# A gated linear recurrence followed by a squared-ReLU feed-forward: GpSimd left out from block 9 on, wider zero products, and another written order

## The chip, the cores and the metric

The kernel runs on one core of one Trainium2 chip. The metric is the device time in microseconds (us). Three runs of the kernel before took 178.39, 179.05 and 180.15 us; their median is 179.05 us. One more execution was profiled: it took 179.38 us by the same clock, and its span from the first to the last instruction is 177.7 us. TensorE's granted clock was 1.00 over that span.

## The reference

```python
# q, k, v, alpha: (4, 8, 768, 48) float32; w_in (384, 2048), w_out (2048, 384), s and b scalars
for t in range(S):
    state = alpha[:, :, t, :, None] * state + einsum('bhd,bhe->bhde', k[:, :, t], v[:, :, t])
    y[:, :, t] = einsum('bhd,bhde->bhe', q[:, :, t], state)
x = y.transpose(0, 2, 1, 3).reshape(B * S, H * D)      # 3072 x 384
h = x @ w_in
r = maximum(h, 0.0)
g = s * (r * r) + b
out = g @ w_out                                         # 3072 x 384, float32
```

## The kernel before

The 3072 rows are cut into 24 blocks of 128 (4 batches of 6 blocks; the state starts anew with each batch). Blocks 0 to 5 are loaded and prepared in pairs with interleaved rows, blocks 6 to 23 one by one. The recurrence of a block is done in chunk form:

- loads `a`, `q`, `k`, `v` (alpha and the three inputs, 192 KB each, rows of 192 bytes; line 172, in pairs line 188), six buffers each, all issued by SyncE (SP);
- `ln` (ScalarE, line 324): log of alpha; `cum` (TensorE, lines 335 to 361): running sums by a triangular matrix into PSUM; `eb`, `ei`, `el` (ScalarE, lines 368 to 386): exponentials of them;
- `qb`, `kb` (helper line 234): q and k times these exponentials, two inputs in SBUF. Blocks 0 to 5 are then transposed on TensorE (`T`, line 417) and copied out of PSUM (`Tc`); the others by a DMA transpose (`Td`) from SP;
- `vc`: v cast to bf16; `KV` (lines 439, 451): k by v; `t` and `sn` (lines 464, 466, 234): the new state; `A` (lines 481, 491): the scores; `mk` (lines 502, 508): their mask, PSUM in, 1.22 us on VectorE; `y`, `ya`, `ys` (lines 530, 544, 561): the output, transposed; `ye`: copied out of PSUM as bf16.

The feed-forward takes two blocks at a time. `m` (line 592, 96 of them) is six products of 256 columns into one PSUM bank; `re` (lines 599, 601) its ReLU, `sq` (lines 609, 234) its square into the SBUF ring `gt` that holds 12 blocks. `w` (line 626, 96 of them, the last four on line 618) is four products of 384 columns, a quarter of one block's output sum; `oe` (line 641) adds scale and bias, `st` stores. The weights come as eight loads of 768 KB: `i0` to `i3` (w_in) and `o0` to `o3` (w_out), cast by `ci` and `co` on whichever engine the order names. `ca` to `cd` and `bm` add up w_out's rows for the bias.

All eight PSUM banks are shared by everything; the tables `H_BANK`, `C_BANK` and so on give the bank of each use. `R_BANK` names one of four buffers between `re` and `sq`.

Nothing is scheduled at run time. `ORDER` is one long text of tokens. Each token is a step and a number, with a letter ahead where it runs on another engine than its default (D VectorE, A ScalarE, P GpSimd, S SyncE, T TensorE). The program emits the steps in this order, so each engine's queue holds its own tokens in the order of the text, and every queue is worked off in order: what stands at the head waits, and all behind it with it. The text was written by a planner outside this file.

`z` (line 659) are products of zeros into a bank that is free then. They give nothing to the result; `FILLS` says how many and how wide. TensorE's first one stands at the head of its queue.

Of the kernel before, what the change touches and what calls it, by code (L numbers as in the profile page):

```python
# [51 lines left out]
qb2 T1 KV1 pq2 pk2 KV0 P:kb3 zvp3 A:Tc1 el2 z4 A1 ya0 P:kb2 vc2 t0 mk1 t1 z5 T3 ys1 ya1 ln4 ln5 T2
cum5 i3 Tc3 A:vc3 ye1 KV3 KV2 ye0 Tc2 sn1 A3 cum4 eb5 A2 t2 el5 ei5 mk3 ci0 P:ci1 zs2 pv2 i1 ys2
el4 eb4 ei4 sn2 m0 m1 mk2 ys3 t3 P:ci5 re1 ya3 ya2 D:ci4 re0 sq0 qb5 ye3 ye2 m5 qb4 m4 m8 m9 P:ci7
o0 re5 re4 a6 A:sq4 A:sq5 kb5 sq1 re8 T5 kb4 m13 re13 T4 Tc5 ci6 A:sq13 m12 A5 D:re9 Tc4 D:of0 mk5
m7 sn3 m6 A:sq8 vc5 m15 s0 D:vc4 D:re12 A:sq9 o3 A4 re6 re7 ci2 KV5 KV4 m14 mk4 ci3 A:sq12 o1 o2
re15 m2 ya5 a8 a7 a9 k7 k6 A:sq15 ya4 ys4 t4 D:sn4 ys5 q6 D:co1 D:re14 P:co0 D:re2 D:ye4 v6 m10 m3
w0 w8 sm0 sq7 ln6 q7 v7 k8 sq6 A:sq14 re3 ye5 re10 U0 m21 m16 A:sq10 m11 re21 A:sq21 co7 sq2 sq3
ca0 se0 D:re16 P:co6 cum6 D:co3 el6 re11 A:sq11 ei6 ca3 sq16 m23 m18 w12 m17 m19 re18 ln8 D:re23
D:co2 re19 eb6 re17 ln7 ca1 D:co5 w4 D:co4 cb0 w9 m20 ca2 cb1 kb6 sq17 A:sq18 w13 A:sq19 cc0 qb6  # L60
cd0 D:re20 a11 a10 m22 cum8 w10 w1 cum7 w5 w11 w2 ei8 el8 eb7 ln9 el7 re22 qb7 w6 w14 bm0 w3 eb8
w7 ei7 A:sq22 be0 oe0 sq23 D:vc6 A:sq20 A:vc7 Td6 P:kb7 w20 w16 KV6 w15 w21 cum9 oe2 Td7 q8 t6
ln10 ei9 ln11 oe1 oe3 eb9 w22 A6 A7 w17 w18 w23 mk6 cum10 mk7 y6 y7 q9 KV7 oe5 D:ye7 k9 v9 v8 q10
k10 w19 eb10 ei10 ye6 el10 cum11 m31 el9 t7 oe4 P:qb8 m26 P:qb9 D:re31 kb8 A:vc8 ei11 m25 m24
D:re25 D:re24 m27 A:sq25 m29 eb11 A:sq24 P:kb9 D:re26 P:qb10 k11 Td9 D:re27 D:vc9 P:kb10 A:sq31
KV8 m30 w24 q11 Td8 w28 re30 KV9 A:sq26 a12 sq30 D:re29 sn7 t8 D:sn8 A:sq27 m28 w25 re28 A:sq28
A:sq29 A9 Td10 v10 A8 w29 t9 w26 ln12 mk9 v11 a13 w27 w30 mk8 cum12 y8 y9 A10 P:kb11 w31 P:qb11
ye8 oe6 sn9 D:vc10 el12 ye9 ln13 mk10 vc11 eb12 m37 KV10 Td11 m34 oe7 m36 t10 q13 k13 cum13 k12
a15 D:re34 A11 re36 re37 mk11 m35 ei12 el13 sq36 m39 eb13 m32 sn10 re39 ei13 a14 q12 q14 y11 v13
qb13 sq39 sq37 kb12 ye11 y10 P:kb13 D:re35 ln15 ye10 D:re32 A:sq35 m38 m33 m46 cum15 D:re33 A:sq32  # L70
m44 A:sq33 a17 D:re46 ln14 D:re38 sq38 m45 m42 w36 m41 cum14 Td13 A:sq46 sq34 el15 D:re42 D:re44
ln17 m40 A:sq44 P:qb12 Td12 k14 v12 w37 re45 el14 w38 w39 ei14 eb15 ei15 D:re40 A13 D:vc13 sq45
oe9 A12 A:sq40 mk12 v14 w32 mk13 m43 w33 re41 sq41 a18 a16 w34 A:vc12 eb14 re43 P:kb14 KV12 A:sq43
v15 m47 q15 sq42 t12 w35 A:vc14 ln16 y13 y12 qb14 ye12 w44 D:ye13 re47 cum17 v19 k15 cum16 oe8 k16
eb16 A:sq47 ei17 KV13 P:qb15 m53 v16 Td14 t13 w40 m48 kb15 D:re48 eb17 ln18 el16 re53 ei16 KV14
m55 w41 m52 D:re55 m50 Td15 A:sq55 re52 m54 P:kb16 vc15 w45 KV15 m51 D:sn13 A:sq48 re54 q17 D:re50
t14 D:vc19 A14 mk14 sn14 A:sq50 A15 mk15 t15 w42 w46 A:sq52 q18 A:sq54 w47 m49 y14 re51 y15 oe11
k19 k17 P:qb17 vc16 D:re49 D:sn15 KV16 w43 q16 ye14 ye15 m59 a19 A:sq49 ln19 A:sq51 sq53 qb16 k18
a20 a21 q20 P:kb17 cum18 m57 oe10 w52 m61 Td16 re57 D:re59 Td17 m56 w53 m58 q19 v17 A:sq57 ei18
sq59 D:re61 v18 cum19 ei19 el19 el18 eb18 w54 t16 m63 re58 A:sq61 w55 m62 D:re63 D:re56 sn16 eb19  # L80
P:kb18 sq58 P:kb19 q21 a22 A16 A17 mk17 oe13 ln20 w48 w49 cum20 k20 k23 vc17 w50 m60 w51 D:re62
# [29 lines left out]
def kernel(  # L111
# [15 lines left out]
    B, H, S, D = q.shape  # L127
# [239 lines left out]
    def o_eb(e, u):  # L367
        e.activation(  # L368
            out=b_sb[u % NB].rearrange("a h d -> a (h d)"), in_=BANK[C_BANK[u]][:, 0:384], func=AF.Exp
        )  # L370

    def o_ei(e, u):
        e.activation(  # L373
            out=binv_sb[u % NB].rearrange("a h d -> a (h d)"), in_=BANK[C_BANK[u]][:, 0:384], func=AF.Exp,
            scale=-1.0,
        )

    def o_el(e, u):
        if u < NPB:
            n, g = u - u % 2, u % 2  # L380
            e.activation(
                out=blast_sb[:, n % NBL : n % NBL + 2, 2 * g : 2 * g + 2],
                in_=BANK[C_BANK[u]][:, 384:388].rearrange("a (p c) -> a c p", c=2), func=AF.Exp,
            )
# [386 lines left out]
```

## Time and profile before

| what | value |
|---|---|
| median of three runs | 179.05 us |
| profiled execution: its time, its span | 179.38 us, 177.7 us |
| VectorE busy | 134.0 us (75%), 239 instructions |
| ScalarE busy | 111.3 us (63%), 242 instructions |
| GpSimd busy | 54.6 us (31%), 83 instructions |
| DMA queue 1 (loads, transposes, stores) | 113684 packets, 34.61 MB |
| DMA queue 8 (instructions) | 18 packets, 0.29 MB |

A line of instruction groups gives the source line, the engine, the operation, output<-inputs, the shapes and xcount, then busy us and mean ns of one, then the idle time of the engine just ahead of it and what ended most of that. A timeline line gives start and length in us, the engine and the operation; in brackets the idle time ahead of it and what ended it ("issue" means nothing that the profile shows). "PEld" is TensorE's loading of weights, which overlaps its products.

### The profile page before, as it was taken

The numbers are of one execution on the slowest core, as the hardware profiler recorded it, in microseconds if no ns is written. First come the engines' busy times: TensorE is split into PE (matmuls) and PEld (weight loads), VectorE is DVE, ScalarE is ACT, GpSimd is POOL, SyncE is SP. The second block draws the span as 40 slices with busy tenths as digits, with TensorE's granted clock in tenths as the row PEclk, the third lists the DMA queues.
The fourth block names the chain that finished last, engine by engine and source line by source line (L and its number), as shares of the span: only waits on it lengthen the run. The fifth ranks groups of instructions, "written<-read, shape, count | busy, mean of one in ns | idle before, by whom it ended". The sixth has DMA issues, their size and how long they took to land.

```text
span 177.7 us, 5545 instructions
## 1 busy us (share of the span) xinstructions
PE 169.5 (95%) x2289; PEld 127.7 (72%) x2289; DVE 134.0 (75%) x239; ACT 111.3 (63%) x242; POOL 54.6 (31%) x83
## 2 busy tenths in 40 slices
PE   7898799899999999999999999999999999999992
PEld 7787597677656786687767868767767688877672
DVE  2298889999977999999887789496978779634421
ACT  3867689798662467367686857559649544956000
POOL 7686512400023715214022352634235302000000
PEclk9999999999999999999999999999999999999999
DMA  5999999999799969999989999999979993000352
GB/s 146 325 318 289 271 329 360 313 280 199 141 224 191 200 144 198 146 203 174 192 171 226 128 209 184 197 210 186 207 127 266 185 344 139 4 0 0 141 208 98
DMA packets 113708, 34.96 MB, mean 197 GB/s; under 512 B 106900, under 2 KB 112148, under 8 KB 113684
## 3 DMA queue, kind: packets, MB, share of 16 engines
q1 hardware_dynamic: 113684, 34.61, 87.8%
q8 instruction: 18, 0.29, 0.7%
q14 instruction: 6, 0.05, 0.1%
HBM read 25.17 MB, written 4.72 MB: 168 GB/s over the span
## 4 chain that ended last, share of the span: by engine, by line
PE 71%; DVE 7%; SPq 7%; ACT 6%; DMA 4%; issue 3%; POOL 1%; DVEq 0%; ACTq 0%
PE bank_ps L626 31%; PE bank_ps L592 28%; SPq L188 5%; DMA wst<-in_moe_w_in_dram 4%; PE bank_ps L481 3%; ACT gt L609 2%; PE bank_ps L544 2%; DVE r L601 2%; ACT r L599 2%; PE bank_ps L335 2%; PE bank_ps L530 2%; SPq L258 2%; PE bank_ps L618 1%; DVE am L502 1%; PE bank_ps L439 1%
## 5 line engine op out<-in xcount | busy, mean ns | idle before, releaser
L592 PE MATMUL bank_ps<-xd,w_in_bf 128*128 128x256 bf16 x576 | 72.0, 273 | 1.8 <-DVE r L601 1.1
L626 PE MATMUL bank_ps<-w_out_bf,gt 128*128 128x384 bf16 x368 | 68.1, 326 | 0.0
L592 PEld LDWEIGHTS <-w_in_bf 128*128 128x128 bf16 x576 | 54.5, 98 | 12.2 <-issue 0.9
L626 PEld LDWEIGHTS <-gt 128*128 128x128 bf16 x368 | 34.5, 98 | 19.5 <-issue 0.2
L599 ACT ACTIVATE r<-bank_ps 128x512 bf16<-128x512 f32 x52 | 30.6, 597 | 16.6 <-PE bank_ps L592 11.9
L609 ACT ACTIVATE gt<-r 128x512 bf16<-128x512 bf16 x61 | 36.8, 628 | 5.4 <-DVE r L601 4.9
L601 DVE TENSOR_SCALAR r<-bank_ps 128x512 bf16<-128x512 f32 x44 | 29.3, 685 | 8.9 <-PE bank_ps L592 6.4
L234 POOL TENSOR_TENSOR qk<-k_in,binv 128x384 bf16<-128x384 f32 x16 | 17.0, 1066 | 39.3 <-ACT binv L373 26.6
L502 DVE TENSOR_TENSOR am<-bank_ps,U_bf 128x1024 bf16<-128x1024 f32 x18 | 21.5, 1220 | 4.1 <-PE bank_ps L481 3.6
L234 DVE TENSOR_TENSOR gt<-r 128x512 bf16<-128x512 bf16 x35 | 17.1, 507 | 3.5 <-ACT r L599 3.3
L641 DVE SCALAR_TENSOR_TENSOR wst<-bank_ps,s_col,bias_w 128x384 f32<-128x384 f32 x23 | 14.0, 614 | 6.9 <-PE bank_ps L626 6.4
L234 POOL TENSOR_TENSOR qk<-q_in,b_s 128x384 bf16<-128x384 f32 x13 | 13.4, 1031 | 17.4 <-DMA q_in<-in_q_dram 13.9
L373 ACT ACTIVATE binv<-bank_ps 128x384 f32<-128x384 f32 x24 | 11.9, 498 | 10.3 <-PE bank_ps L342 7.7
L234 POOL TENSOR_TENSOR s_st<-t,blast 128x384 bf16<-128x384 bf16 x11 | 9.4, 855 | 23.7 <-DVE t L466 23.6
L229 ACT ACTIVATE xd<-bank_ps 128x384 bf16<-128x384 f32 x19 | 9.4, 520 | 9.8 <-PE bank_ps L544 9.2
L324 ACT ACTIVATE la<-a_in 128x384 bf16<-128x384 f32 x24 | 12.3, 522 | 5.1 <-DMA a_in<-in_alpha_dram 5.1
L368 ACT ACTIVATE b_s<-bank_ps 128x384 f32<-128x384 f32 x24 | 12.0, 499 | 4.5 <-PE bank_ps L342 3.4
L466 DVE TENSOR_TENSOR t<-bank_ps,s_st 64x192 bf16<-64x192 f32 x32 | 11.3, 352 | 1.7 <-POOL s_st L234 0.6
L234 DVE TENSOR_TENSOR qk<-q_in,b_s 128x384 bf16<-128x384 f32 x11 | 6.0, 550 | 6.3 <-DMA q_in<-in_q_dram 5.9
L659 PE MATMUL bank_ps<-zeros 128*128 128x128 bf16 x81 | 7.2, 255 | 1.3 <-DVE half_bf L695 1.3
L508 DVE TENSOR_TENSOR am<-bank_ps,maskp 128x1024 bf16<-128x1024 f32 x6 | 7.3, 1223 | 0.7 <-PE bank_ps L491 0.6
L530 PE MATMUL bank_ps<-qkT,s_st 128*32 128x128 bf16 x240 | 6.8, 221 | 0.6 <-issue 0.6
(87 smaller groups left out, 156.9 us busy)
## 6 DMA issues: line engine op xcount, KB each, us to landing
out_dram<-wst SPq DMA_DIRECT2D x23, 192.0 KB, 3.1
a_in<-in_alpha_dram SPq DMA_DIRECT2D x18, 192.0 KB, 4.4
k_in<-in_k_dram SPq DMA_DIRECT2D x18, 192.0 KB, 3.9
q_in<-in_q_dram SPq DMA_DIRECT2D x18, 192.0 KB, 3.8
v_in<-in_v_dram SPq DMA_DIRECT2D x18, 192.0 KB, 3.8
wst<-in_moe_w_in_dram SPq DMA_DIRECT2D x4, 768.0 KB, 7.5
wst<-in_moe_w_out_dram SPq DMA_DIRECT2D x4, 768.0 KB, 7.6
a_in<-in_alpha_dram SPq DMA_DIRECT2D x3, 384.0 KB, 4.8
```

What stands on the lines that cost most here:

```text
L234: e.tensor_tensor(out=o, in0=x, in1=y, op=ALU.mult)
L324: e.activation(out=la_sb[u % NLA].rearrange("a (r h) d -> a r h d", r=2)[..., 0:D], in_=seen("a", u), func=AF.Ln,)
L368: e.activation(out=b_sb[u % NB].rearrange("a h d -> a (h d)"), in_=BANK[C_BANK[u]][:, 0:384], func=AF.Exp)
L373: e.activation(out=binv_sb[u % NB].rearrange("a h d -> a (h d)"), in_=BANK[C_BANK[u]][:, 0:384], func=AF.Exp, scale=-1.0,)
L466: e.tensor_tensor(out=t1_sb[n % 2][r, :, c], in0=kv[r, :, c], in1=s_sb[(n - 1) % 3][r, :, c], op=ALU.add,)
L502: e.tensor_tensor(out=am.rearrange("a e p t -> a (e p) t"), in0=a_ps.rearrange("a e p t -> a (e p) t"), in1=U_bf.unsqueeze(1).to_broadcast ...
L592: nc.tensor.matmul(out=hp[:, i * 256 : (i + 1) * 256], lhsT=w_in_bf[:, kk, 128 * j : 128 * (j + 1)], rhs=xd_sb[g % 3][:, kk, :], start=(kk ...
L599: e.activation(out=r_sb[R_BANK[w]], in_=BANK[H_BANK[w]], func=AF.Relu)
L601: e.tensor_scalar_max(r_sb[R_BANK[w]], BANK[H_BANK[w]], 0.0)
L609: e.activation(out=o, in_=r, func=AF.Square)
L626: nc.tensor.matmul(out=BANK[bank][:, 0:d_model], lhsT=gt_sb[:, j, c0 : c0 + C], rhs=w_out_bf[:, j, :], start=(j == 0), stop=(j == NJ - 1),)
L641: e.scalar_tensor_tensor(out=out_sb[n % NOS], in0=BANK[O_BANK[n]][:, 0:d_model], scalar=s_col[:, 0:1], in1=bias_w, op0=ALU.mult, op1=ALU.add,)
```

## The change

Three things change together. The names of banks and buffers are drawn anew, and `ORDER` is another text with the same steps. From block 9 on no step is given to GpSimd. `FILLS` now gives a number of columns and the widest product, and `o_z` cuts the columns into products of up to that width: 13184 columns in 28 products, where there were 10368 columns in 81. The planner that wrote the order also counted TensorE's instruction pages and their packets among the loads; nothing of that shows in the code but the order itself.

The steps that change engine (all others have the same count on the same engine):

| step | before | after |
|---|---|---|
| `kb` | VectorE 8, GpSimd 16 | VectorE 20, GpSimd 4 (blocks 2, 3, 4, 7) |
| `qb` | VectorE 11, GpSimd 13 | VectorE 20, GpSimd 4 (blocks 1 to 4) |
| `sn` | VectorE 5, GpSimd 11 | VectorE 14, GpSimd 2 |
| `vc` | ScalarE 8, VectorE 8, GpSimd 8 | ScalarE 17, VectorE 3, GpSimd 4 |
| `re` | ScalarE 52, VectorE 44 | ScalarE 61, VectorE 35 |
| `sq` | ScalarE 61, VectorE 35 | ScalarE 52, VectorE 44 |
| `ye` | ScalarE 19, VectorE 5 | ScalarE 16, VectorE 8 |
| `Tc` | ScalarE 1, VectorE 5 | ScalarE 2, VectorE 4 |
| `ci` | ScalarE 4, VectorE 1, GpSimd 3 | ScalarE 3, VectorE 3, GpSimd 2 |
| `co` | ScalarE 1, VectorE 5, GpSimd 2 | ScalarE 3, VectorE 3, GpSimd 2 |

The core of the diff:

```diff
-FILLS = [(0, 32, 128), (1, 12, 128), (1, 4, 128), (1, 15, 128), (7, 12, 128), (7, 6, 128)]
+FILLS = [(0, 4288, 512), (0, 1792, 512), (1, 1536, 512), (6, 512, 512), (7, 2304, 512), (1, 384, 512), (5, 448, 512), (2, 960, 512), (4, 960, 512)]
...
 def o_z(e, x):
-        bank, m, w = FILLS[x]
-        for _ in range(m):
+        bank, cols, step = FILLS[x]
+        while cols:
+            w = min(cols, step)
             nc.tensor.matmul(
                 out=BANK[bank][:, 0:w], lhsT=zeros[:, 0:128], rhs=zeros[:, 0:w], start=True, stop=True
             )
+            cols -= w
```

TensorE's own tokens, from the head of the order to the first `w`. Before:

```text
z0 cum0 cum1 z1 cum2 cum3 z2 T0 z3 A0 T1 KV1 KV0 z4 A1 ya0 z5 T3 ys1 ya1 T2 cum5 KV3 KV2 A3 cum4 A2
ys2 m0 m1 ys3 ya3 ya2 m5 m4 m8 m9 T5 m13 T4 m12 A5 m7 m6 m15 A4 KV5 KV4 m14 m2 ya5 ya4 ys4 ys5 m10 m3 w0
```

After:

```text
z0 cum0 cum1 z1 cum3 z2 T0 cum2 T1 KV0 A0 z3 A1 KV1 z4 T3 ys1 ya0 z5 ya1 T2 A3 z6 KV2 KV3 A2 cum5
m0 ys2 z7 cum4 ya3 ya2 z8 m5 m4 ys3 m1 m9 T5 m12 m8 A5 T4 m6 m7 A4 KV5 KV4 m15 sm0 m13 m11 ys4 ys5
ya5 ya4 m3 m2 m20 m22 m18 m14 m10 m23 w12
```

SP's tokens up to the load `a8`. Before: `pa0 pk0 pa1 pq0 pv0 pq1 pk1 pa2 pv1 i0 i2 pq2 pk2 i3 pv2 i1 o0 a6 s0 o3 o1 o2 a8`. After: `pa0 pq0 pa1 pk0 pv0 pq1 pk1 pv1 pa2 i0 i2 pk2 pq2 i3 pv2 i1 s0 o0 o3 o1 o2 a6 a7 a8`. Behind that the single loads and the transposes stand in other places too; the last load of v is `v23` before (93 transfers behind `a8`) and `v22` after (86 behind).

TensorE's program has 4585 instructions before and 4476 after, VectorE's 322 and 348, ScalarE's 304 and 317, GpSimd's 138 and 72.

More of the change, by code (lines that the diff above doesn't have):

```diff
@@ L52 @@
[L52 to L69, printed above, removed]
@@ new lines @@
+1, 1, 3, 3, 0, 2, 2, 1, 0, 0, 1, 2, 0, 3, 0, 0, 1, 2, 1, 0, 2, 3, 1, 2, 3, 0, 3, 3, 2, 0, 0, 1, 3,
+0]
+FILLS = [(0, 4288, 512), (0, 1792, 512), (1, 1536, 512), (6, 512, 512), (7, 2304, 512), (1, 384, 512), (5, 448, 512), (2, 960, 512), (4, 960, 512)]
+ORDER = """
+zz0 P:zqk1 Us0 D:zs2 id0 zvp2 sml0 pre0 zla1 Ui0 P:zla0 pa0 zqk0 D:zt1 zt0 ln0 mp0 D:zvp1 z0 cum0
+ln1 cum1 el0 pq0 pa1 eb0 eb1 ln3 pk0 ei0 ei1 zqk2 qb0 P:qb1 D:zvp0 pv0 el1 z1 cum3 eb3 ln2 A:vc0
+pq1 kb0 z2 T0 ei3 kb1 cum2 T1 pk1 el3 pv1 Tc0 Tc1 pa2 el2 eb2 ei2 i0 vc1 i2 KV0 A0 mk0 z3 A1 KV1
@@ new lines @@
+zs0 zvp3 P:qb3 pk2 P:kb3 pq2 z4 T3 A:vc3 P:kb2 A:Tc3 t0 ys1 ya0 D:zs1 mk1 z5 ya1 P:qb2 vc2 T2 t1
+A3 ye0 ye1 z6 KV2 KV3 P:ci0 D:sn1 mk3 A:Tc2 A2 t2 ln5 ci1 mk2 cum5 m0 ys2 D:sn2 i3 ln4 z7 cum4 ya3
+ya2 t3 pv2 D:ci5 ei5 D:zvp5 D:ci4 eb4 eb5 re0 ei4 i1 el4 z8 m5 kb5 P:kb4 ye2 D:of0 m4 ys3 m1 ye3
+A:sq0 m9 el5 re1 D:re5 qb5 sq5 T5 re4 m12 Tc5 D:re9 A:sq4 D:ci6 P:qb4 sn3 zvp4 vc5 re12 m8 ci7 A5
+P:ci3 re8 A:sq8 s0 T4 o0 A:vc4 m6 m7 Tc4 A4 KV5 re6 A:sq12 KV4 o3 mk5 sq1 t4 A:sq9 m15 sm0 m13 mk4
+m11 D:re13 se0 sq6 re15 ci2 sn4 ys4 o1 o2 ys5 ya5 ya4 a6 P:co0 a7 m3 re7 m2 A:sq7 D:ye5 sq13 re11
@@ new lines @@
+sq11 sq15 ye4 m20 m22 re3 re2 A:sq3 a8 m18 A:sq2 m14 D:re22 sq22 co1 m10 m23 re14 co6 D:re20 ca0
+w12 sq14 re10 m17 A:sq10 P:co2 D:re18 w8 D:co7 m16 ca3 k6 a9 q8 co3 re17 A:sq17 ln6 A:sq20 D:co4
+D:co5 w0 m19 U0 w13 cum6 ca2 w1 ca1 eb6 ei6 w2 cb0 cb1 el6 w4 k7 cc0 w5 re19 sq19 ln7 re23 cum7
+ei7 q6 eb7 w14 w15 w9 m21 q7 cd0 ln8 k8 sq18 qb6 re16 bm0 w6 kb6 qb7 v6 P:kb7 be0 cum8 re21 A:sq16
+w7 v7 a11 vc6 Td6 oe3 ei8 eb8 ln9 w3 w10 w11 A:vc7 oe0 Td7 q9 w20 el7 KV6 cum9 v8 oe1 oe2 k9 t6
+kb8 v9 eb9 w16 w21 qb8 KV7 w17 ln11 el8 el9 t7 A6 mk6 A:sq21 ei9 A7 A:sq23 mk7 w18 qb9 kb9 w19
@@ new lines @@
+cum11 w22 oe4 D:sn7 D:vc8 eb11 ei11 y6 y7 ye6 Td8 a10 ye7 A:vc9 w23 m28 m25 re25 a12 Td9 KV8 m30
+A8 oe5 ln10 m24 re30 a13 cum10 m26 A:sq25 re28 mk8 ln12 t8 D:re26 m31 A9 ei10 D:sn8 k12 v10 k10
+m27 el10 re24 A:sq30 m29 q11 mk9 sq24 k11 y8 y9 w24 sq28 ln13 eb10 A:sq26 D:ye9 ye8 re27 D:re29
+KV9 m37 q10 re31 t9 D:re37 A:sq29 a17 m33 m39 A:sq31 sq27 kb10 m38 m36 re33 A:vc10 re39 cum12 w28
+w25 m32 cum13 qb11 kb11 qb10 v11 q12 sq33 D:sn9 re36 el12 m34 KV10 w26 A:sq36 ei12 Td11 eb12 Td10
+eb13 w29 m35 re32 re38 A:sq37 ei13 w27 a15 w30 kb12 sq39 a14 sq32 D:re34 el13 A:sq34 k13 A11 t10
@@ new lines @@
+m54 w46 w47 re53 ln18 m51 a20 t14 D:re52 D:sn14 w41 A15 kb16 oe11 ei17 D:re51 A:vc16 A:vc15 eb17
+A14 m50 A:sq52 m48 w42 mk15 re54 mk14 D:re48 y15 y14 k17 ye15 A:sq51 sq48 q17 q16 D:ye14 cum18
+kb17 q18 qb17 A:sq53 el18 eb18 w43 KV15 t15 qb16 oe10 qb18 m57 m56 D:sn15 re50 m60 A:sq50 k18 v17
+v20 a19 A:sq54 w52 ei18 w48 D:vc17 D:re56 KV16 m61 Td16 m59 A:sq56 w53 Td17 D:re61 D:re57 v21 k19
+kb18 ln19 re59 A:sq57 A:sq59 re60 m58 re58 w49 w54 t16 w50 cum19 A17 A16 D:sn16 eb19 A:sq61 m62
+Td18 v18 w51 w55 mk16 mk17 A:sq58 el19 ln20 w60 y16 oe13 y17 re62 oe12 ei19 ye17 m63 D:ye16 sq62
@@ new lines @@
+w56 q19 a21 q20 D:re63 sq60 qb19 kb19 m68 m65 m70 m64 st6 a22 v19 Td19 A:vc20 cum20 A:vc18 re70
+el20 re65 sq65 ln21 A:sq63 q22 m69 w61 D:re64 D:re69 sq70 eb20 ei20 A:vc21 w57 w58 v23 D:re68
+A:sq68 k20 KV18 w62 w59 k23 t18 A19 A:sq64 A18 A:vc19 mk19 m66 ln22 mk18 sq69 m67 re66 oe14 sq66
+a23 w63 cum21 re67 w68 y18 kb20 ei21 y19 cum22 qb20 D:ye18 oe15 m71 eb21 k21 st1 st10 A:sq67 q21
+ye19 el21 eb22 el22 ei22 ln23 re71 KV19 w69 KV20 m73 t19 m72 cum23 sq71 D:sn19 q23 k22 w70 m76 w64
+eb23 D:re73 re72 A:sq73 re76 kb21 qb21 m79 w71 ei23 t20 sq72 kb22 m75 v22 Td20 KV21 m74 re75 sq76
```

71 lines of the change are left out of this document (27 added, 44 removed).

## The prediction

> **What bounds the kernel now.** I read the page first (busy times, slices), then a table of stages, then what TensorE waits for, then GpSimd's waits.
>
> ```profile
> PE 169.5 (95%) x2289; PEld 127.7 (72%) x2289; DVE 134.0 (75%) x239; ACT 111.3 (63%) x242; POOL 54.6 (31%) x83
> ...
> PE   7898799899999999999999999999999999999992
> ```
>
> ```profile
> 24.70:34.40 9.70, 8.96 (x195) 7.14 (x193) 8.61 (x15) 8.67 (x17) 3.65 (x7) 1.00 1.03 325
> 34.40:51.20 16.80, 16.80 (x131) 12.10 (x131) 15.47 (x27) 14.32 (x31) 2.12 (x2) 1.00 0.96 223
> 51.20:100.00 48.80, 47.98 (x619) 35.00 (x618) 42.19 (x73) 29.34 (x68) 14.92 (x16) 1.00 1.02 182
> 100.00:150.00 50.00, 50.00 (x661) 37.42 (x660) 40.06 (x69) 31.27 (x68) 17.64 (x22) 1.00 1.04 207
> ```
>
> Columns: stage, length, busy PE, PEld, VectorE, ScalarE, GpSimd, clock, DMA share, GB/s. TensorE is never free from 34 us to the end, and its products stand at their closest spacing there: six of an `m` take 0.656 us, four of a `w` 0.65 us, start to start. So the time is TensorE's work, which the change leaves alone, plus what it loses. It loses 1.25 us before the first product, about 6.3 us in zero products, a tail of 3.4 us behind the last product, and the waits below (start to start beyond the spacing).
>
> ```profile
> 7.31 0.32 PE L348 MATMUL bank_ps<-la,Ui_bf 128*128 128x384 bf16 x1 [0.52 <-ACT blast L381]
> ...
> 16.79 0.42 PE L491 MATMUL bank_ps<-qkT 64*64 64x128 bf16 x16 [0.46 <-ACT xd L229]
> ...
> 20.36 0.35 PE L530 MATMUL bank_ps<-qkT,s_st 128*32 128x128 bf16 x12 [0.57 <-issue]
> ...
> 22.08 2.79 PE L592 MATMUL bank_ps<-xd,w_in_bf 128*128 128x256 bf16 x24 [0.62 <-POOL w_in_bf L231]
> ...
> 34.40 0.82 PE L592 MATMUL bank_ps<-xd,w_in_bf 128*128 128x256 bf16 x6 [0.74 <-DVE r L601]
> ...
> 73.02 0.41 PE L544 MATMUL bank_ps<-am,vp 128*32 128x128 bf16 x16 [0.43 <-DVE am L502]
> ...
> 82.39 0.83 PE L592 MATMUL bank_ps<-xd,w_in_bf 128*128 128x256 bf16 x6 [0.39 <-DVE r L601]
> ```
>
> Start to start, the last three cost 0.91, 0.60 and 0.56 us. All three come from VectorE, behind an operation that stood still while GpSimd ran:
>
> ```profile
> 32.28 1.34 DVE L231 CAST w_out_bf<-wst 128x768 bf16<-128x768 f32 x1
> ...
> 66.67 1.25 DVE L234 TENSOR_TENSOR gt<-r 128x512 bf16<-128x512 bf16 x1
> ...
> 78.79 0.41 DVE L234 TENSOR_TENSOR gt<-r 128x512 bf16<-128x512 bf16 x1
> ...
> 80.37 1.36 DVE L234 TENSOR_TENSOR qk<-k_in,binv 128x384 bf16<-128x384 f32 x1
> ```
>
> The same `sq` takes 0.41 us alone and 1.25 us beside two GpSimd products (66.64 to 68.78); a cast of w_out takes 0.55 alone, `kb` 0.55. Over the run seven `sq`, two `kb`, one `sn` and that cast lose 5.6 us so. ReLUs and masks, which read PSUM, do not (0.685 either way).
>
> **The change part by part.**
>
> *Zero products.* 81 products of 10368 columns become 28 of 13184. The first runs at half rate (107 ns per 128 columns): 4288 columns take 3.58 us against 3.41, so `cum0` starts at 4.83 instead of 4.80. The other 8896, at the 56 ns per 128 columns of the later ones, take 3.9 us against 2.7. A product of 512 columns is not in the trace; the bf16 one of 384 takes 0.162 us, the same per column. I cost the 1.2 us more at nothing: `z3` to `z8` stand where TensorE waits for casts and masks. Without that cover it is +1.2.
>
> *The start, to `T5`.* The loads keep their places up to `i2`, except that q of pair 0 now comes second and k fourth (about 5.4 and 7.9 us, the landings of those places). So `kb0` runs at 8.0 and `T0` at 8.55, as before (8.57). `T1` follows at 9.6 (10.33) and `A1` at 11.0 (12.10). Then GpSimd makes `qb3`, `kb3`, `kb2`, `qb2` one after another, 1.0 to 1.4 us each, from 10.4: `T2` at 15.0 (14.62). `Tc3` and `Tc2` go to ScalarE (1.02 us against 0.69), with `vc3` and both `ye` ahead of `Tc2`: `A2` at 17.65 after a wait of about 0.85, `m0` at 18.65 (18.31) with `cum4` and `ys2` (0.75 us) still to do. The next gate is `i2`, which lands at 20.9 in both: `ci5` on VectorE gives `m5` at about 21.8 (22.08), and then `m4 ys3 m1 m9`, so `T5` at 24.4 against 24.71. But `m8` (0.66) is not done yet: 0.3 us behind. Hand chain of some thirty steps; I allow 1 us either way.
>
> *Instruction pages.* Queue 8 brings TensorE's instructions, 18 packets of 16 KB, so 256 instructions each. In the packet records they start when TensorE passes each 256th instruction, but at 13.9 us it passes and the packet starts only at 17.90; 256 instructions on, exactly at `ys3`, TensorE stands still until 20.36 with nothing to wait for. So the page took 6.4 us; the others came in at most 4 to 6. After the change the same place is passed at about 16.1 and the page is needed at 21.3 (in `ya2`): nothing, or up to 1.2 us. I take 0, the nearer to the other pages. The Trainium skill ("Runtime: NRT & Kernel Launch", Instruction fetch mechanics) has the crossing of a 16 KiB boundary "mostly hidden"; the row at 20.36 speaks against it. By that rule the sum stays as it is; by the row's 6.4 us it would be 1.2 higher.
>
> *From `T5` to the first `w`.* The cast that stood still 0.8 us at 32.28 made `re14` late and cost TensorE 0.91 before `m3`. In the new order no cast of w_out runs on VectorE until `co7`, ten or so steps later, but `co0`, `co2` and the mask `U0` still run on GpSimd beside VectorE's `sq`. I take -0.7, with ends -0.9 and 0.
>
> *The rest.* VectorE gets 12 `kb`, 9 `qb`, 9 `sn`, 3 `ye` at 0.47 us (back-to-back spacing) and 9 `sq` at 0.34, and loses 9 `re` at 0.60, 5 `vc` at 0.27 and one `Tc` at 0.61: +11.2 us, less most of the 5.6 us of standing still, so about 140 us busy. ScalarE: +9 `re` at 0.49, -9 `sq` at 0.52, +9 `vc` at 0.41, -3 `ye` at 0.39, casts and `Tc` +1.7: +3.9, so 115 us. In 51 to 150 us VectorE goes from 83% to some 88%; TensorE stays the bound and covers both. The waits at 73.02 and 82.39 go: -1.2, ends -1.2 and 0. VectorE's fuller queue brings others, such as `y14` behind two masks: +0.3, ends 0 and +1.2. The tail is as before: after the last `m` ten `w` follow while VectorE needs about 4 us for the last ReLUs and squares, 2.6 us of `w` stand ahead of the first that needs one, and a store of 96 KB ends both.
>
> Sum: 179.38 + 0.3 + 0 - 0.7 - 1.2 + 0.3 = 178.1. The profiled execution lies 0.33 above the median, so 177.8.
>
> **The rivals.**
>
> *Loads late at the head of VectorE's queue (slower).* GpSimd has stood waiting for q and k, at no cost to TensorE:
>
> ```profile
> POOL qk L234 <- DMA q_in<-in_q_dram: 13.9, 4, 5.1
> POOL qk L234 <- DMA k_in<-in_k_dram: 8.1, 3, 3.3
> ```
>
> Now `kb` and `qb` wait on VectorE, with ReLUs, squares and masks behind them, and TensorE behind those. From `a8` (lands 40.3) to `v23` (144.3) 93 transfers land, 1.12 us each. With that spacing, and TensorE's work ahead of each step plus 11.5 us, loads land before their use by 0 us (`k9`), 0.4 to 0.6 (`a14`, `a15`, `v14`), 0.9 (`k22`, `q18`), in the middle 4.1. Before, the same reckoning gives -2.6 for the worst and 2.2 in the middle, so the new order is safer, which speaks against this rival. It decides from about 0.5 us lateness on at `k9`, or a spacing of 1.2 us: then each microsecond of lateness reaches TensorE. 2 to 4 us of it give 181. The rule in the Trainium skill that speaks against the change is that VectorE and ScalarE work their queues strictly in order ("TensorE: Matmul & The Clock Gate", Architectural detail). The trace agrees: VectorE stood 5.91 us for q before 7.96, with casts that were ready behind it.
>
> *The gain is given back (same).* Page late (+1.2) or zeros uncovered (+1.2): 179.0. For it: the start is tight. Against: TensorE waits there anyway.
>
> *The start goes better (faster).* `T1` and `A1` come 0.7 and 1.1 us earlier; if `T2` and `A2` follow, 1.5 us more go: 176.3. Against: GpSimd's four products in a row.
>
> *It does nothing.* If the three waits were not from GpSimd, the moved work only fills VectorE and the time stays at 179: counted with the second.
>
> **How the numbers follow.** Forecast 0.38 (177.1 to 178.6), late loads 0.22, given back 0.22, better start 0.18. A measurement of this kernel can tell about 1% from no change: below 177.3 is faster, above 180.8 slower. Faster: the better start and half of the forecast's case, 0.37. Slower: most of the late loads, 0.18. Same: 0.45. Range 175.9 to 181.0.
>
> **What would show it.** Right: `sq` and `kb` after 50 us all near 0.41 and 0.55; no TensorE wait on VectorE of over 0.3 us between 50 and 100; `T5` near 24.4 to 24.9, the first `w` near 38. Wrong: VectorE waiting for q, k or v loads; an "issue" gap on TensorE near 21; TensorE under 9 tenths after 35 us; `m5` behind 23.

## The result, and the profile after

The changed kernel takes 179.75 us (median of 20 runs, 179.33 to 180.53), the kernel before 178.87 (20 runs, 178.12 to 180.15): a ratio of 1.0056, interval 1.0039 to 1.0072. So it is about 0.5% slower, by more than the noise; the forecast was 177.8. Ratios and intervals, here and below, leave out executions that ran over 1.5% longer than the fastest one of their kernel; the medians in us do not. The profiled execution of the changed kernel took 179.47 us, with a span of 177.6.

From the page of the changed kernel, the busy times and TensorE's slices:

```profile
PE 170.3 (96%) x2233; PEld 124.5 (70%) x2236; DVE 142.2 (80%) x268; ACT 115.0 (65%) x251; POOL 21.6 (12%) x45
...
PE   7998699999999999999999999999999999999992
```

VectorE (142) and ScalarE (115) came out near the 140 and 115 that were forecast. The table of stages, with the columns as before:

```profile
24.70:34.40 9.70, 9.70 (x200) 7.86 (x200) 8.10 (x14) 9.54 (x20) 3.58 (x7) 1.00 0.80 242
34.40:51.20 16.80, 16.61 (x132) 12.04 (x130) 15.36 (x26) 13.67 (x27) 3.95 (x5) 1.00 1.02 241
51.20:100.00 48.80, 48.80 (x632) 35.61 (x631) 42.84 (x81) 34.81 (x82) 0.03 (x1) 1.00 0.96 185
100.00:150.00 50.00, 50.00 (x648) 36.59 (x646) 43.34 (x82) 32.50 (x72) 0.00 (x0) 1.00 0.96 202
```

TensorE's gaps in the first and third row (9.70 - 8.96 and 48.80 - 47.98 before) are closed; one of 0.19 us is new in the second. So the waits that the change should remove are gone, and yet the kernel is slower. What TensorE waited for in the changed kernel, from its timeline:

```profile
16.85 0.42 PE L491 MATMUL bank_ps<-qkT 64*64 64x128 bf16 x16 [0.36 <-ACT qkT L229]
...
18.14 0.83 PE L592 MATMUL bank_ps<-xd,w_in_bf 128*128 128x256 bf16 x6 [0.33 <-POOL w_in_bf L231]
...
21.57 0.23 PE L561 MATMUL bank_ps<-am,vp 64*32 64x128 bf16 x3 [0.69 <-issue]
21.97 0.35 PE L660 MATMUL bank_ps<-zeros 128*128 128x448 bf16 x1 [0.16 <-issue]
22.16 1.47 PE L592 MATMUL bank_ps<-xd,w_in_bf 128*128 128x256 bf16 x12
...
25.27 0.61 PE L417 MATMUL bank_ps<-ident_bf,qk 128*128 128x128 bf16 x8
...
40.71 0.81 PE L626 MATMUL bank_ps<-w_out_bf,gt 128*128 128x384 bf16 x4 [0.19 <-DVE r L601]
```

A2 and m0 start earlier than forecast (16.85 and 18.14 against 17.65 and 18.65). Then TensorE stands in ya2 until 21.57 with nothing to wait for, the zero products z8 follow (0.42 us; one of the two is missing in this trace), m5 starts at 22.16 and T5 at 25.27 (forecast 21.8 and 24.4). The casts of w_in that m5 and m4 need were done on VectorE before that, at 20.83 and 21.49:

```profile
20.14 0.69 DVE L231 CAST w_in_bf<-wst 128x768 bf16<-128x768 f32 x1
...
20.86 0.63 DVE L231 CAST w_in_bf<-wst 128x768 bf16<-128x768 f32 x1
```

So in this order m5 stands behind the stop in ya2 and behind z8, and no longer behind the load of w_in. At 40.71 there is a wait ahead of w8 that the kernel before does not have.

To compare orders that do the same work in another sequence I use a **lag**: the time at which TensorE starts a step, less the time that all it has done so far would take at its closest spacing (m 0.656, w 0.65, a y 0.40 and so on, zero products nothing; 157.93 us in all for either order). Both kernels were profiled a second time (below). In the order first trace, second trace:

| | before | changed | change of the mean |
|---|---|---|---|
| lag at T5 | 10.85, 10.54 | 12.07, 12.07 | +1.4 |
| more of it up to 46 us | 1.11, 1.12 | 0.56, 1.01 | -0.3 |
| more from there to the last product | 4.64, 4.36 | 3.50, 3.74 | -0.9 |
| last product to the end of the span | 3.12, 3.13 | 3.52, 3.52 | +0.4 |
| outside the span | 1.68, 1.62 | 1.87, 2.00 | +0.3 |

The sum is +0.9 us, as the medians have it. The gain of the middle came; the start took more than it, and the end, which no term of the forecast touched, took 0.7 more. The two traces of one kernel end TensorE's work 0.6 and 0.7 us apart, so a row holds to a few tenths.

### The profile page after: what moved, and what is told of

Same layout as the page of the kernel before. It is cut to its first block, busy times and chain, and to the rows that moved or that the text cites. A ratio compares the mean times of both kernels' runs of the same rounds, so it can differ in the third digit from the quotient of the medians.

```text
span 177.6 us, 5399 instructions
## 1 busy us (share of the span) xinstructions
PE 170.3 (96%) x2233; PEld 124.5 (70%) x2236; DVE 142.2 (80%) x268; ACT 115.0 (65%) x251; POOL 21.6 (12%) x45
## 4 chain that ended last, share of the span: by engine, by line
PE 89%; DVE 3%; issue 3%; POOL 2%; ACT 1%; DVEq 0%; POOLq 0%
PE bank_ps L626 34%; PE bank_ps L592 34%; PE bank_ps L481 3%; PE bank_ps L660 3%; PE bank_ps L530 2%; PE bank_ps L544 2%; PE bank_ps L335 2%; POOL qk L234 2%; PE bank_ps L618 1%; PE bank_ps L439 1%; PE bank_ps L417 1%; PE bank_ps L561 1%; DVE r L601 1%; PE bank_ps L348 1%; PE bank_ps L342 1%
## 5 line engine op out<-in xcount | busy, mean ns | idle before, releaser
L599 ACT ACTIVATE r<-bank_ps 128x512 bf16<-128x512 f32 x61 | 35.4, 595 | 16.2 <-PE bank_ps L592 12.4
L609 ACT ACTIVATE gt<-r 128x512 bf16<-128x512 bf16 x52 | 31.6, 628 | 5.5 <-DVE r L601 5.2
L601 DVE TENSOR_SCALAR r<-bank_ps 128x512 bf16<-128x512 f32 x35 | 23.8, 687 | 8.3 <-ACT gt L609 3.2
L234 DVE TENSOR_TENSOR gt<-r 128x512 bf16<-128x512 bf16 x44 | 19.4, 453 | 5.1 <-ACT r L599 4.8
L234 DVE TENSOR_TENSOR qk<-q_in,b_s 128x384 bf16<-128x384 f32 x20 | 11.1, 561 | 4.0 <-ACT b_s L368 4.0
L234 DVE TENSOR_TENSOR qk<-k_in,binv 128x384 bf16<-128x384 f32 x20 | 10.9, 550 | 1.5 <-DMA k_in<-in_k_dram 1.0
L229 ACT ACTIVATE vp<-v_in 128x384 bf16<-128x384 f32 (+1 forms) x20 | 8.9, 469 | 1.9 <-DMA v_in<-in_v_dram 1.9
L660 PE MATMUL bank_ps<-zeros 128*128 128x512 bf16 (+4 forms) x25 | 8.0, 446 | 1.6 <-DVE zeros L702 1.3
L234 DVE TENSOR_TENSOR s_st<-t,blast 128x384 bf16<-128x384 bf16 x14 | 7.8, 561 | 0.2
L544 PE MATMUL bank_ps<-am,vp 128*32 128x128 bf16 x288 | 7.0, 219 | 0.0
```

What stands on the lines that cost most here:

```text
L229: e.activation(out=o, in_=i, func=AF.Copy)
L234: e.tensor_tensor(out=o, in0=x, in1=y, op=ALU.mult)
L599: e.activation(out=r_sb[R_BANK[w]], in_=BANK[H_BANK[w]], func=AF.Relu)
L601: e.tensor_scalar_max(r_sb[R_BANK[w]], BANK[H_BANK[w]], 0.0)
L609: e.activation(out=o, in_=r, func=AF.Square)
L660: nc.tensor.matmul(out=BANK[bank][:, 0:w], lhsT=zeros[:, 0:128], rhs=zeros[:, 0:w], start=True, stop=True)
```

## The experiments

The theory after the first trace (START) was that the order of the start costs what the middle gains, above all since m1 and ys3, which the kernel before does while it waits for w_in, now stand behind m5. Against it stood CHANCE (the first trace of the kernel before was an unusual execution) and ZEROS (the wider zero products). Further on came END and OUT, on the last microseconds, and ENGINES, on what moving work off GpSimd is worth. Ratios are to runs of the kernel before on the same chip.

**The kernel before once more.** No edit.

> The kernel before, unchanged, for a second trace and the spans of its own executions. Three theories stand. START: the waits at y8, m46 and ahead of m3 (0.60, 0.56 and 0.91 us in the first trace) are there in every execution and went with the change, and the change lost about 1.25 us again before T5 (m1 and ys3 now stand behind the wait for w_in) and 0.4 in the tail; then the median is 178.9 and the second trace shows the three waits again with a sum of 1.7 to 2.2 us. CHANCE: the first trace, 0.5 us above the median, was an unusual execution, and the three waits are mostly its own; then their sum is under 1.0 us here. ZEROS: the wider zero products are what the change costs; it says nothing of this run (178.9).

Measured: 178.79 us, ratio 1.0001 (0.9974 to 1.0029). From its timeline of TensorE:

```profile
72.44 0.41 PE L544 MATMUL bank_ps<-am,vp 128*32 128x128 bf16 x16 [0.38 <-DVE am L502]
...
81.80 0.83 PE L592 MATMUL bank_ps<-xd,w_in_bf 128*128 128x256 bf16 x6 [0.39 <-DVE r L601]
```

The waits at y8 and m46 are there again (0.55 us each, start to start); the one of 0.91 ahead of m3 is not, and another of 0.92 at ya4 stands in its place, 0.70 of it with nothing to wait for. The sq and the kb that stood still ahead of the two did so again (1.11 and 1.35 us). CHANCE holds for the one and falls for the two.

**Three cuts between the two orders.** One kernel takes the order of before up to T5 and then what is left in the changed order; one does so up to 46 us; a third takes the changed order up to ye4 (33 us) and then that of before.

```diff
 ORDER = """
-  (changed order, all of it)
+  (order of before up to T5, or up to re20) + (changed order, what is not yet done)
```

> Up to T5 the order, the banks and the zero products of the kernel before, behind it the changed order with what is not yet done. START: the 1.25 us lost before T5 are gone, 178.5 us (178.2 to 178.9), and the waits at y8, m46 and of 0.9 ahead of m3 stay away. CHANCE: the changed order is slower in the middle or at the end, so the start changes little: 179.4 to 179.8. ZEROS: the products of zeros are again those of before (10368 columns), so also about 178.6; the run with tiny zero products tells this from START.

> Up to 46 us (re20, m22) the order of the kernel before, behind it the changed order. Only the two waits of VectorE in the middle (1.16 us) and the tail differ from the kernel before. START: 178.9 - 1.2 + 0.4 = 178.1 us (177.8 to 178.4). CHANCE: no gain is left in the middle and the tail is longer: 178.9 to 179.4. ZEROS: nothing in the middle comes from zeros, so as START, 178.1.

> The changed order up to ye4 (33 us on TensorE), behind it the order of the kernel before, with GpSimd's steps from block 9 on as there. START: the 0.7 to 1.0 us that the changed order loses in its first 33 us stay, and the waits at y8 and m46 come back: 179.4 to 180.0. Rival: the loss of the changed order lies behind 33 us: 178.6 to 178.9.

Measured: 179.63 us (1.0074, 1.0044 to 1.0103), 179.07 (1.0020, 0.9995 to 1.0045), 186.96 (1.0448, 1.0398 to 1.0497). Two of the three cuts have a wait of their own where the two orders meet (a seam). First what TensorE waited for with the start of before:

```profile
PE bank_ps L302 <- DMA sb_row<-in_moe_b_dram: 1.1, 1, 1.1
```

then what ScalarE waited for with the changed start:

```profile
ACT la L318 <- DMA a_in<-in_alpha_dram: 9.5, 4, 6.8
```

The small load s0 came late in the one, the load a6 (6.8 us, at 34 to 41 us) in the other. So their times say nothing of START; both were badly chosen. Their traces still tell of the middle: behind 51 us the changed order adds a lag of 3.51, the order of before 4.34, with the waits at y8 and m46 (0.52 and 0.56). That is 0.8 us between the two orders, in kernels with other starts. The cut at 46 us, without such a seam, ends TensorE's work at 173.33 against 173.95 and 174.54 of before, and gives some of it back behind the last product: 3.54 us to the end of the span against 3.13. But this was one of its faster executions (178.58 us). Behind 51 us it adds 3.7. Its median lies 0.7 us above START's range and in that of CHANCE, and the same order with five memsets (below) ended TensorE's work at 174.29. So the medians of this cut do not bear out the 0.8 us that the traces give for the middle.

**Zero products of two columns.** The same 19 products of z1 to z8, of 2 columns each:

```diff
-FILLS = [(0, 4288, 512), (0, 1792, 512), (1, 1536, 512), (6, 512, 512), (7, 2304, 512), ...]
+FILLS = [(0, 4288, 512), (0, 8, 2), (1, 6, 2), (6, 2, 2), (7, 10, 2), ...]
```

> The changed kernel, with every product of zeros behind the first group (z1 to z8, 19 products, 8896 columns, 3.9 us at 56 ns per 128 columns) cut to 2 columns; the same number of instructions, and nothing of the result depends on them. START: they stand where TensorE waits anyway, so the time stays at 179.6 to 179.9 as long as the clock stays up. ZEROS: the part that is not covered goes, 178.0 to 178.8. A third way: the clock falls in the gaps, TensorE's first products run at 107 ns per 128 columns for longer, and the time is 180.5 to 183.

Measured: 179.73 us (1.0079, 1.0050 to 1.0109), TensorE's last product at 174.12 against 174.06, m0 at 18.18 against 18.14. ZEROS falls as the cause of the lost time: taking out 3.9 us of zero products wins nothing. But they don't all lie in waits. Without the columns of z8, m5 follows the stop in ya2 at once:

```profile
21.80 1.47 PE L586 MATMUL bank_ps<-xd,w_in_bf 128*128 128x256 bf16 x12
```

So m5 and T5 (24.90) come 0.36 us earlier than in the changed kernel; w8 does not (40.76 against 40.71), and there the 0.36 us are lost again. Nor did the clock fall in the profiled execution (0.999).

**Only the engines.** In the changed order 35 steps (kb, qb, sn and vc from block 9 on) go back to GpSimd; in the order of before the same 35 leave it.

```diff
-... kb10 ... qb11 kb11 qb10 ... D:sn9 ...
+... P:kb10 ... P:qb11 P:kb11 P:qb10 ... sn9 ...
```

> The changed order with kb, qb, sn and vc of blocks 9 on given back to GpSimd wherever the kernel before has them there (35 steps, only the letter of the engine). ENGINES: VectorE stands still beside GpSimd again, waits of 0.5 us and more appear between 50 and 150 us, 1.0 to 2 us more TensorE time there; against this the end of GpSimd's program moves (0.5 less if END holds): 180.2 to 181.3. Rival: the engine of these steps is worth nothing: 179.2 with END, 179.7 without.

> The order of the kernel before, unchanged, with the same 35 steps moved from GpSimd to VectorE and ScalarE (only the letter of the engine). ENGINES: the waits at y8 and m46 go, 178.8 - 1.1 = 177.7 (177.4 to 178.0), if GpSimd's program does not end at a page of instructions; 0.5 more if it does. Rival: VectorE's 13.6 us of new work in an order not made for it bring waits of their own: 178.5 to 180.5.

Measured: 179.83 us (1.0075, 1.0047 to 1.0103) and 187.34 us (1.0430, 1.0363 to 1.0497). With the engines back, from the table of stages:

```profile
51.20:100.00 48.80, 48.80 (x631) 35.59 (x630) 38.38 (x70) 34.22 (x81) 12.49 (x13) 1.00 1.07 185
100.00:150.00 50.00, 50.00 (x648) 36.57 (x645) 36.36 (x65) 31.01 (x68) 19.22 (x21) 1.00 0.98 204
```

GpSimd works 32 us there again, and TensorE is as full as without: a lag of 3.50 behind 46 us, to the hundredth that of the changed kernel. VectorE's squares, in the view of one tile (least, median and longest in ns), first of the changed kernel, then with the engines back:

```profile
L234 DVE TENSOR_TENSOR gt<-r x44: 401/418/1219, 24.3 to 169.3; 128x512 bf16<-128x512 bf16 x44
```

```profile
L228 DVE TENSOR_TENSOR gt<-r x44: 401/424/1223, 24.6 to 169.4; 128x512 bf16<-128x512 bf16 x44
```

Three squares of the changed kernel take over 0.5 us, the last at 48.2 us; with the engines back it is seven, four of them behind 50 us (0.58 to 0.94 us), and two kb of 0.63 and 0.68. VectorE does stand still again, if less than in the kernel before (five squares from 60 us on, up to 1.25, and two kb and one sn of 0.94 to 1.36), but TensorE does not wait for it. The times agree only loosely. The measured 179.83 lies between the rival's 179.2 and ENGINES' 180.2 to 181.3; the trace is of its fastest execution (179.21), and the end of this kernel is 0.5 us shorter (below), so its median would allow 0 to 0.7 us for the engines, the trace allows none. The changed kernel with five memsets at 15 us (below), on the same chip and with the same short end, has nearly the same ratio, 1.0076.

In the order of before the move costs 4.3%, 7.7 us. Its profiled execution was its longest (189.56 us, at a clock of 0.991), so only the kind of its waits is read here. The longest of TensorE's, then what VectorE waited for ahead of it:

```profile
137.35 0.32 PE L329 MATMUL bank_ps<-la,U_bf 128*128 128x384 bf16 x1 [2.12 <-DVE r L595]
```

```profile
136.14 0.56 DVE L228 TENSOR_TENSOR qk<-k_in,binv 128x384 bf16<-128x384 f32 x1 [1.84 <-DMA k_in<-in_k_dram]
```

This is my first rival, a late load at the head of VectorE's queue, in an order that was not made for it. It is not all of it: three waits are for DMA transposes, 2.4 us together:

```profile
PE bank_ps L475 <- DMA qkT<-qk: 2.4, 3, 1.1
```

So the gain of the middle does not need an idle GpSimd: by the trace the new order, with its banks and buffers, has it with GpSimd at work too, though VectorE's standstills are then smaller than in the order of before. That the order keeps more between a step and its use is a guess. Whether the two waits of the order of before would go without the standstills, these two runs do not show, since the moved steps bring larger waits there.

**The end of GpSimd's program.** Five memsets more, once at 15 us, once behind its last step, and once in the order cut at 46 us:

```diff
-P:qb2 vc2 T2 t1
+P:qb2 vc2 zvp4 zvp4 zvp4 zvp4 zvp4 T2 t1
```

> The changed kernel with five more memsets on GpSimd, all of one region of vp4 that it zeroes anyway, put where GpSimd waits for i0 (15.2 to 17.2 us); nothing else. In the traces so far GpSimd's last steps stand differently: in the kernel before its last DRAIN starts 0.04 us behind the clearing of the semaphores and takes 0.03, in the changed kernel 0.37 behind it and takes 0.17, with every engine waiting for it, and the time outside the span is 1.85 us against 1.65. END: GpSimd's shorter program ends where a page of its instructions ends, so the last ones come late; five instructions more move the end away from there: the last matmul to the end of the span falls from 3.54 to 3.1 us, the time to 179.1 to 179.3. IDLE: GpSimd is slow to start again because it was idle for 120 us; then nothing changes, 179.6 to 179.9. START says nothing of the end.

```diff
-a11 vc6 Td6
+a11 vc6 of0 of0 of0 of0 of0 Td6
```

> The changed kernel with five more memsets on GpSimd behind its last step (of ones_f, which nobody reads any more; about 52 us), nothing else. With five memsets at 15 us the tail became 0.5 us shorter in the trace, but the median did not move, and those memsets held GpSimd for 1.5 us just ahead of the cast of w_in. END: here nothing else is touched, so the last matmul to the end of the span falls from 3.54 to 3.05 us and the median to 179.2 to 179.4. Rival: the late end of GpSimd is made up for elsewhere, or counts in no median: 179.6 to 179.9.

> The order of the kernel before up to 46 us, the changed order behind it, and five memsets behind GpSimd's last step. Without them it took 1.0020 of the kernel before (0.9995 to 1.0045) with a tail of 3.54 us. END: tail 3.05, 0.5 us less, 0.998 to 1.0005. Rival: as without them, 1.001 to 1.003.

Measured: 179.71 us (1.0076, 1.0045 to 1.0107), 179.82 (1.0039, 1.0009 to 1.0068) and 179.15 (1.0000, 0.9971 to 1.0029).

**The end of ScalarE's program.** el22 nine times:

```diff
-el22
+el22 el22 el22 el22 el22 el22 el22 el22 el22
```

> The changed kernel with el22, a step of 0.05 us on ScalarE, done nine times instead of once (about 125 us). In every trace of a kernel with 315 instructions of ScalarE a page of 8 KB of instructions comes in 1.7 to 1.95 us behind the end of the span, and the time outside the span is 1.87 to 1.99 us; with 300 to 314 there is none, and 1.62 to 1.75. OUT: ScalarE's program ends at a page; with eight more the page comes in earlier, unseen, the time outside the span is 1.62 to 1.75, 0.2 us less. Rival: it is TensorE's or another engine's program, and nothing changes (1.8 to 2.0).

Measured: 180.65 us (1.0095, 1.0059 to 1.0132). The repeats were not free: the eight held ScalarE for 1.67 us, 0.21 each and not 0.05, and TensorE waited behind them (0.63 us at m72, start to start):

```profile
PE bank_ps L586 <- ACT binv L367: 0.5, 1, 0.5
```

The end itself reads the same way in every trace. "Records" are the instructions of an engine in the trace; the late page is a packet of 8 KB of instructions that starts 1.75 to 1.95 us behind the end of the span:

| kernels | GpSimd records | ScalarE records | last product to span's end | outside the span, median | late page |
|---|---|---|---|---|---|
| before (both) | 137 | 302 | 3.12, 3.13 | 1.66 | no |
| cut at 46 us | 71 | 307 | 3.54 | 1.73 | no |
| changed (both), tiny zeros | 71 | 315 | 3.52 to 3.54 | 1.80 to 1.95 | yes |
| engines back | 138 | 315 | 3.06 | 1.94 | yes |
| five memsets (both) | 75, 76 | 315 | 3.05, 3.06 | 1.93, 1.98 | yes |
| cut at 46 us, five memsets | 76 | 307 | 3.04 | 1.73 | no |
| el22 nine times | 71 | 323 | 3.54 | 1.70 | no |

In the kernels with 71 records GpSimd's last DRAIN starts 0.37 us behind the clearing of the semaphores and takes 0.17; with 75 and more 0.04 and 0.03. All engines wait for it. The packets of instructions move with the counts. With 71 records one of 8 KB starts 0.29 to 0.48 us behind the end of the span in all seven traces; with five memsets more there is none, and one at 45 to 56 us in its place. ScalarE's late page goes to 11 to 12 us ahead of the end with eight instructions more. Kernels that the table leaves out agree; the one with the 35 steps moved in the order of before has 74 records and 3.44 us. So the number of instructions decides, not GpSimd's idle 120 us: in the traces END and OUT hold, at 0.5 and 0.2 to 0.25 us.

The medians are less clear. The two memset kernels of the changed order missed END's times (179.71 and 179.82 against at most 179.4); by the ratios the 0.5 us (0.3%) show as 0.2% in two of the three memset kernels, within the noise of each, and not at all in the one with memsets at 15 us. The profiled executions of the two on the changed order had late loads (m0 at 19.71 and 19.25 in place of 18.14); whether those memsets cost something of their own stays open.

**m1 and ys3 early, ca0 late.** Both undo what the changed order does in its first 46 us:

```diff
-z7 cum4 ya3 ya2 ... z8 m5 kb5 P:kb4 ye2 D:of0 m4 ys3 m1 ye3
+z7 cum4 m1 ys3 ya3 ya2 ... z8 m5 kb5 P:kb4 ye2 D:of0 m4 ye3
```

> The changed kernel with m1 and ys3 put ahead of ya3 and ya2, where the kernel before has them, and so ahead of the wait for w_in at m5 and of the instruction page that ya2 waits for (1.13 us at 20.39); m1 gets another bank (1 in place of 0). START: 0.7 to 0.9 us of the wait are filled with work, 178.9 to 179.1, and ya2's wait falls under 0.5. Rival: the page is asked for later by as much as it is needed later, or cum4's followers come late, and nothing is gained: 179.6 to 179.9.

Measured: 179.34 us (1.0038, 1.0012 to 1.0064). From its timeline, m1, ys3, ya3 with ya2, and m5:

```profile
20.41 0.82 PE L586 MATMUL bank_ps<-xd,w_in_bf 128*128 128x256 bf16 x6
21.15 0.35 PE L524 MATMUL bank_ps<-qkT,s_st 128*32 128x128 bf16 x12
21.43 0.82 PE L555 MATMUL bank_ps<-am,vp 64*32 64x128 bf16 x64
...
22.60 2.13 PE L586 MATMUL bank_ps<-xd,w_in_bf 128*128 128x256 bf16 x18
```

The stop in ya2 is gone, filled with m1: 0.4 us less lag at T5 (11.64 against 12.07). The time lies between START's range and the rival's. By 46 us the lag is 12.59, against 12.63 and 13.08 of the changed kernel: w8 still starts at 40.67. In the seven traces with ca0 early and no late loads it starts at 40.67 to 41.17, whether T5 came at 24.84 or 25.28.

```diff
-D:re20 ca0 w12 ... D:re18 w8 D:co7 m16
+D:re20 w12 ... D:re18 w8 D:co7 ca0 m16
```

> m1 and ys3 early, as in the run before with m1 (179.34), and also ca0, an addition of 0.95 us for the bias, moved on VectorE from ahead of sq14 to behind co7: re18, which w8 waits for, comes 0.9 us earlier. START: the wait at w8 (0.35 to 0.77 us in the traces of this order) goes, 178.8 to 179.0. Rival: something behind it is as late (a cast of w_out, whose load lands at 37 to 40 us): 179.2 to 179.5.

> The changed kernel with m1 and ys3 early, ca0 late and the five memsets behind GpSimd's last step. If START and END both hold, 0.4 + 0.5 + 0.5 us go: 178.3 to 178.6, faster than the kernel before (178.75) and than the changed one (179.75). Without END 178.8 to 179.0; without the wait at w8 178.8.

Measured: 179.66 us (1.0032, 1.0006 to 1.0058) and 178.73 (0.9992, 0.9961 to 1.0023). The wait at w8 is gone in both traces (it starts at 39.95 in the first, with a lag at 46 us of 11.88, as in the kernel before), but the first had 0.85 us at A9, behind a DMA transpose, in its profiled execution, and its median won only 0.1% over m1 alone.

**Everything together.** First beside the changed kernel itself, then with ScalarE's repeats where it has nothing left to do:

> The changed kernel once more, beside the others of this call on the same chip: 1.0056 times the kernel before (1.0039 to 1.0072), a tail of 3.5 us behind the last matmul, 1.8 to 1.9 us outside the span, waits at ya2 (about 1.1 us) and at w8 (0.35 or more) and none of over 0.3 us between 50 and 150 us.

> The changed kernel with m1 and ys3 early, ca0 late, five memsets behind GpSimd's last step and el22 nine times. The three without el22 gave 0.9992 of the kernel before (0.9961 to 1.0023). With OUT 0.2 us more: 0.996 to 1.000, 178.2 to 178.7 beside 178.9 of before, and 0.9 to 1.5 us below the changed kernel of this call. Rival: the three causes do not add up, 1.001 to 1.004.

Measured: 180.21 us (1.0069, 1.0039 to 1.0098) and 179.21 (1.0001, 0.9969 to 1.0033); the second has the 0.63 us of el22 at m72 in it. In the second trace of the changed kernel, from its timeline:

```profile
21.57 0.23 PE L561 MATMUL bank_ps<-am,vp 64*32 64x128 bf16 x3 [0.68 <-issue]
...
41.16 0.81 PE L626 MATMUL bank_ps<-w_out_bf,gt 128*128 128x384 bf16 x4 [0.64 <-DVE r L601]
```

The stop in ya2 came back to the hundredth, the wait at w8 larger.

```diff
-re94 sq94
+re94 ln23 ln23 ln23 ln23 ln23 ln23 ln23 ln23 sq94
```

> The changed kernel with five memsets behind GpSimd's last step and eight repeats of ln23 (0.45 us each, nobody reads them) behind ScalarE's last step, from 166 us on, where ScalarE is idle. END and OUT: tail 3.05 in place of 3.52, 1.70 in place of 1.9 us outside the span, together 0.7 us: 1.0020 of the kernel before (1.000 to 1.004), where the changed kernel has 1.0056 and 1.0069. Rival: the shorter end counts in no median, 1.005 to 1.007.

> The same with m1 and ys3 early and ca0 late. START with END and OUT: waits at ya2 and w8 under 0.4 us, nothing at m73, 0.9957 to 0.998 of the kernel before, and 0.3 to 0.9 us below the kernel with the ends alone. Rival: the causes do not add up, 1.000 to 1.003.

Measured: 179.36 us (1.0031, 1.0012 to 1.0049) and 178.66 (0.9979, 0.9960 to 0.9997). The ends alone are worth 0.25 to 0.4% (0.5 to 0.7 us by the parts: 3.06 and 1.73 in place of 3.52 and 1.8 to 1.95). The two edits to the start bring 0.5% more, on one chip and clear of noise: every one of the twelve runs is below the lowest of the other kernel. How much each of the two brings is not told apart; in this trace T5 came late again (a lag of 12.11, with 0.71 us behind kb5), and the gain stands at w8 (40.42 against 41.05). The last kernel is the changed one without the three losses found, and just faster than the kernel before.

## Why the prediction was wrong

- **Zero products: 0.** Right in the time: 3.9 us of them taken out changed nothing. Not right for z8: the cast that was to cover it was done at 20.83, and its 0.42 us delayed m5. That this cost nothing in the end is owed to w8, which waits for VectorE.
- **The start, to T5: +0.3.** This step failed first: it is +1.4 (12.07 against 10.85 and 10.54). The chain was near enough up to m0 (18.14, forecast 18.65). Behind it I had m5 at 21.8, on VectorE's cast, and T5 2.6 us later. The cast came in time; m5 stood behind the stop in ya2 and z8 instead and began at 22.16. And m5, m4, ys3, m1 and m9 need 4 x 0.656 + 0.27 = 2.9 by my own spacings, and took 3.1. I did not see that m1 and ys3, 0.93 us of work that the kernel before does while it waits for w_in, are missing there in the new order. Putting them back took the stop away and 0.4 us of the lag at T5, but by itself little of the lag at 46 us.
- **Instruction page in ya2: 0.** Wrong, though the place was right, and the issue gap near 21 us was one of the signs I had named: TensorE stood 0.69 and 0.68 us there. The packet of that page started at 19.17 and TensorE went on at 21.57, where before it was 17.90 and 20.36: 2.4 and 2.5 us behind the packet. For this page the sentence of the Trainium skill that I weighed ("Runtime: NRT & Kernel Launch", Instruction fetch mechanics: a crossing is "mostly hidden") does not hold in either kernel's trace; the other 16 pages of the changed kernel show no such stop.
- **From T5 to the first w: -0.7.** It is -0.3. The cast that stood still is gone, but a new wait of 0.35 to 0.8 us stands ahead of w8, behind ca0 and re18 on VectorE. I had reckoned with the casts alone.
- **The waits at 73.02 and 82.39: -1.2, new ones +0.3.** The size was right by the traces (-0.9). The reason, "All three come from VectorE, behind an operation that stood still while GpSimd ran", is not shown: the gain stays with GpSimd at work in the new order, and the order of before with GpSimd idle has larger waits of another kind. So the gain came with the order as a whole, and the size was partly luck. The third of the three waits was one of that execution.
- **"The tail is as before."** It was 0.4 us longer, and the time outside the span 0.2 to 0.3. I compared the last products and stores, and not the lengths of the programs, though I had them: 138 instructions against 72 on GpSimd, 304 against 317 on ScalarE.
- **Late loads, the first rival**, did not come in this order: no wait of TensorE behind VectorE of over 0.3 us between 50 and 150 us. Given back, the second, was nearest (179.0), with the page, and with the zeros at z8 alone. My reading that casts stood ready on VectorE behind the wait for q before 7.96 was wrong: v of that pair landed at 9.05, and only memsets could have run.
- **Squares and kb after 50 us at 0.41 and 0.55**: right, and no sign of the time: with slower ones, given back to GpSimd, TensorE's lag was the same.

The forecast was -1.3 against the profiled execution; terms as measured give 1.4 - 0.3 - 0.9 + 0.4 + 0.3 = +0.9.

What stays open: what in GpSimd's end takes the 0.5 us (the packet of instructions that goes with it starts only 0.3 us or more behind the end, too late to be what the engines wait for), how much of the 0.9 us in the middle is owed to which steps or banks of the new order, and why the cut at 46 us shows so little of it in its medians. The load order of the start was not tried by itself.

## What to carry to other kernels

A wait that ends with a slowed operation isn't shown to be caused by the slowing: move the engine letters alone, in either order, before believing it. When a change alters how many instructions an engine has, look at the last records of each engine and at the time outside the span, for half a microsecond can come or go there with five instructions. When an order moves work past a gate, add up what is done ahead of the gate in both orders; an engine that waits there anyway loses all that was taken from in front of it. And follow a gain to the next wait: 0.4 us won at T5 did not outlast w8 while VectorE was late there.

## What the hardware showed beyond that

- The loads of the first 15 us differ between executions of nearly the same start: k of pair 0 landed at 7.76 to 8.69, and m0 began at 18.06 to 19.71 us, in the 14 traces with the changed start. Not all of that reaches the end: with m0 at 19.25 the lag at 46 us was 12.9, no more than in traces with m0 at 18.1; with m0 at 19.71 it was 14.1.
- TensorE's stop for an instruction page stands at one place of its program, whatever the order: about the 705th record, in 14 of the 20 traces, 0.16 to 1.12 us long, and 512 records on in four (0.30 to 1.10). It ends 2.3 to 2.6 us behind the start of a packet of 16 KB (2.5 to 2.7 at the second place). At the other pages, of 17 or 18 in a run, there is no stop of 0.2 us. In the five kernels with m1 and ys3 early, and in one with late loads, there is none.
- Eight repeats of a ScalarE step of 0.05 us took 1.67 us and cost TensorE 0.63 us at 136 us, while 4.4 us of repeats at 166 us cost nothing that shows.
